# Windowed attention with global tokens, then a squared-ReLU feed-forward layer: matmul width in batch 1, a fourth output buffer, and the order of sums in 256-token chunks

## The chip, the cores and the metric

The kernel runs on one core of a Trainium2 chip. A core has five engines that run side by side[...]: TensorE (PE in the profile, with its weight loads listed apart as PEld), VectorE (DVE), ScalarE (ACT), GpSimd (POOL) and SyncE (SP), which here only issues DMAs. Sixteen DMA engines move data between HBM and the on-chip memory (SBUF). TensorE writes its results to PSUM[...]. The metric is the device time of one execution in microseconds (us); lower is better.

## The reference

Queries, keys and values have 8 batches, 8 heads, 576 tokens and 64 elements per head. A token attends to tokens within 32 positions; 8 global tokens attend to all and are attended by all.

```python
scores = scale * np.matmul(q, k.transpose(0, 1, 3, 2))
mask = np.abs(pos[:, None] - pos[None, :]) <= window        # window = 32
mask = mask | is_global[:, None] | is_global[None, :]
scores = np.where(mask, scores, -1000000000.0)
attn = np.exp(scores - np.max(scores, axis=-1, keepdims=True))
attn_out = np.matmul(attn / (np.sum(attn, axis=-1, keepdims=True) + 1e-09), v)
x = attn_out.transpose(0, 2, 1, 3).reshape(B * S, H * D)    # 4608 x 512
h = x @ w_in                                                # 512 x 2048
r = np.maximum(h, 0.0)
out = (r * r) @ w_out                                       # 2048 x 512
```

## The kernel before

**Attention.** The work is cut into 32 items: item i is a pair of heads of one batch, four items to a batch (`NHP`). Each item has two halves of 288 queries. For an item's half, `sc_mm` (matmuls at L765) makes scores of keys by queries, a head on each 64 rows of the array; `sc_exp` (L774) takes the exponential on ACT, `sc_mask` (L784) multiplies by the 0/1 mask on DVE; `pv_mm` (L806) makes the products with the values and with ones, a head on each 64 columns of the array; `pv_rec`, `pv_sum` and `pv_mul` (L816 to L847) divide and write the result, transposed, into `xT`. `scatter` (L868, POOL) puts in the columns of the global tokens. In batches 0 and 1 keys and queries are loaded as rows and turned round on TensorE by `transpose` (L487; a small product at L493, recorded as L293, picks the global rows); in half 0 of batch 1 the mask is added on TensorE, as a product of `far` with the identity. From batch 2 on, keys and queries go through a scratch in HBM (`kscr`, `qscr`) and come back through transposing DMAs (L201, L202) issued on SP; values come by DMAs on POOL (L207).

**Feed-forward.** The tokens are cut into ten chunks, eight of 512 tokens and two of 256, chunk 4 and the last, chunk 9. `mm1` and, for chunk 0, `mm1_half` multiply by `w_in`; ACT takes the ReLU (`rl`, L538), DVE squares it (`gt`, L540). For chunk 0, `mm2` multiplies by `w_out` directly: four results of 128 tokens, each in four parts; the last part copies the result from PSUM to the tile `ot` (L589) and stores it (L591). All later chunks use `mm2_fast`, which needs seven half-size products in place of eight, in the order 3, 4, 5, 2, 1, 6, 7. Products 5, 2, 1, 6 and 7 read sums or differences of blocks of `gt`, made by `g_sum` on DVE (L625, in tile `mix`) at places that `SUMS` and `SUMS_HALF` set: each entry names the step after which a sum is issued. In `SUMS_HALF` steps 8 to 14 are the seven products. Products are put together by `combine` (L657 into `pt`, L660 into `ot` with a store); product 6 adds onto the bank of product 3 and product 7, in chunk 4, onto that of product 4, so each waits until a combination has read that bank.

**Order.** Every engine takes its instructions in the order in which the program writes them. The attention items set the frame; between their steps `fill(n)` takes feed-forward steps from one list, so that TensorE has work while ACT and DVE do exponentials and masks. A step is only taken when its tokens' batches are done. At the end `take` empties the list. In PSUM, `at` has two buffers of two banks and, from L989 on, `mm` has four of one bank. `ot` has three buffers in SBUF, used in turn.

**How a matmul is issued.** `halves` (L291) issues each product as two matmuls of 64 columns of weights, one for each half of the output's partitions. `transpose` does the same. All such matmuls are recorded under L293 and L487.

## Time and profile before

| | |
|---|---|
| median of 9 runs | 333.19 us (329.68 to 338.06) |
| the profiled execution | 330.38 us |
| its span, first to last instruction | 328.7 us |
| granted TensorE clock, mean | 0.994 |
| PE busy | 309.7 us, 94% of the span |
| DVE, ACT, POOL busy | 244.7, 202.3, 127.1 us |
| DMA moved | 39.35 MB, 120 GB/s |

A line of the profile's groups or timeline names the engine, the line of the kernel, the operation, the tile written and the tiles read, the shape as partitions x elements, and how many. In the timeline the first two numbers are the start and the length in us; a bracket holds the engine's idle time before it and what ended that wait: another engine's instruction, a DMA, or "issue" where nothing in the profile released it. Matmuls overlap, so the busy time of a group is less than its count times its mean. "128*64" is a matmul with 128 rows and 64 columns of weights. In a table of stages a line gives the stretch and its length, then busy time and number of instructions for PE, PEld, DVE, ACT and POOL, the granted clock, the busy share of DMA (where queues overlap it can be over 1) and GB/s.

### The profile page before, as it was taken

The page shows a single profiled execution, that of the slowest core. Times are in us where ns is not written, and L with a number is a line of the kernel's source. Part 1 is how long each engine was busy: PE and PEld are TensorE (multiplying, and loading weights), DVE is VectorE, ACT ScalarE, POOL GpSimd, SP SyncE. Part 2 cuts the span into 40 slices and gives each one's busy share as a digit, 9 for nine tenths or more (in the row PEclk, how much of TensorE's full clock was granted, in tenths as well). Part 3 has the DMA queues.
Part 4 walks back from the last instruction along what each step waited for, and adds up shares of the span by engine and source line. Part 5 has one row for each costly group of instructions (what it writes and reads, how often), then busy time and mean ns, then how long its engine had stood idle before and what let it go on. Part 6 is the DMA issues. An engine that isn't in the chain of part 4 may idle for free.

```text
span 328.7 us, 12010 instructions
## 1 busy us (share of the span) xinstructions
PE 309.7 (94%) x5015; PEld 238.0 (72%) x5015; DVE 244.7 (74%) x601; ACT 202.3 (62%) x380; POOL 127.1 (39%) x222
## 2 busy tenths in 40 slices
PE   7887898998999999999999899999999999999995
PEld 4667786554578758875899756985698569868994
DVE  6783768557898778677867769876987698768465
ACT  3683776544865686668557288658765876363150
POOL 8468767348800960189100970039502000100000
PEclk9997999999999999999999999999999999999999
DMA  8999999999992999499924699469996401200211
GB/s 192 176 182 202 199 190 154 155 117 176 155 118 61 175 157 130 71 177 147 142 79 103 57 181 139 40 130 172 139 98 116 125 0 35 94 5 2 89 45 64
DMA packets 149921, 39.35 MB, mean 120 GB/s; under 512 B 133124, under 2 KB 149300, under 8 KB 149868
## 3 DMA queue, kind: packets, MB, share of 16 engines
q0 software_dynamic: 95408, 16.78, 66.9%
q1 hardware_dynamic: 54042, 21.23, 35.9%
q8 instruction: 39, 0.64, 0.8%
q10 hardware_dynamic: 418, 0.59, 0.7%
q14 instruction: 14, 0.11, 0.1%
HBM read 37.86 MB, written 17.29 MB: 168 GB/s over the span
## 4 chain that ended last, share of the span: by engine, by line
PE 38%; DMA 22%; issue 22%; DVE 7%; POOL 5%; ACT 3%; SPq 1%; POOLq 0%; DVEq 0%
PE mm L293 34%; DMA early<-in_v_dram 9%; DMA w_in<-in_moe_w_in_dram 4%; DMA qscr<-in_q_dram 3%; PE at L806 2%; ACT er L774 2%; PE at L765 2%; POOL xT L868 2%; DMA qt<-qscr 2%; DVE mix L625 2%; DMA gscr_q<-gstq 2%; DMA stf<-in_v_dram 2%; DVE early L619 1%; DVE gt L540 1%; DMA out_dram<-ot 1%
## 5 line engine op out<-in xcount | busy, mean ns | idle before, releaser
L293 PE MATMUL mm<-xT,w_in 128*64 128x512 f16 (+1 forms) x1280 | 123.0, 347 | 2.1 <-DVE ot L589 1.3
L293 PEld LDWEIGHTS <-w_in 128*64 128x64 f16 x1408 | 82.0, 111 | 46.3 <-issue 5.8
L538 ACT ACTIVATE rl<-mm 128x512 f16<-128x512 f32 x128 | 75.0, 598 | 37.5 <-PE mm L293 35.5
L293 PEld LDWEIGHTS <-mix 128*64 128x64 f16 x1280 | 68.5, 110 | 3.5 <-DVE mix L625 1.7
L540 DVE TENSOR_TENSOR gt<-rl 128x512 f16<-128x512 f16 x128 | 52.8, 421 | 22.4 <-ACT rl L538 21.1
L868 POOL COPY xT<-gx 128x4 f16 x64 | 17.7, 277 | 133.4 <-DVE xT L847 130.0
L774 ACT ACTIVATE er<-at 128x880 f16<-128x880 f32 x54 | 46.1, 903 | 15.0 <-PE at L765 13.4
L625 DVE TENSOR_TENSOR mix<-gt 128x1024 f16<-128x1024 f16 (+1 forms) x82 | 53.1, 671 | 0.2
L293 PE MATMUL mm<-early,mix 128*64 128x256 f16 x768 | 45.8, 273 | 1.2 <-DVE mix L625 1.2
L784 DVE TENSOR_TENSOR et<-er,mask 128x880 f16<-128x880 f16 x54 | 33.2, 617 | 17.8 <-ACT er L774 17.3
L816 ACT ACTIVATE rec<-at 128x288 f32<-128x288 f32 x64 | 25.8, 403 | 27.2 <-PE at L806 22.1
L293 PEld LDWEIGHTS <-gt 128*64 128x64 f16 x640 | 34.4, 110 | 8.5 <-DVE gt L540 2.2
L847 DVE TENSOR_TENSOR xT<-at,rec 128x288 f16<-128x288 f32 x60 | 27.1, 451 | 9.1 <-ACT rec L817 8.5
L293 PE MATMUL mm<-early,gt 128*64 128x256 f16 x512 | 32.2, 274 | 1.0 <-DVE gt L540 1.0
L293 PE MATMUL mm<-w_out,mix 128*64 128x256 f16 x512 | 30.9, 273 | 0.0
L806 PE MATMUL at<-et,onesb 128*64 128x192 f16 (+5 forms) x400 | 29.9, 225 | 0.0
L817 ACT ACTIVATE rec<-rec 128x288 f32<-128x288 f32 x64 | 28.4, 443 | 2.0
L660 DVE TENSOR_TENSOR ot<-mm,pt 128x512 f32<-128x512 f32 (+1 forms) x36 | 22.7, 631 | 8.1 <-ACT pt L685 6.7
L178 POOL DMA_DIRECT2D kscr<-in_k_dram x30 | 26.3, 1052 | 3.3 <-DMA w_out<-in_moe_w_out_dram 3.0
L185 POOL DMA_DIRECT2D qscr<-in_q_dram x24 | 23.9, 1398 | 0.6 <-issue 0.6
L806 PEld LDWEIGHTS <-onesb 128*64 128x64 f16 x400 | 22.0, 110 | 1.0
L685 ACT COPY pt<-mm 128x512 f32<-128x512 f32 (+1 forms) x18 | 9.7, 540 | 20.6 <-PE mm L293 20.6
(119 smaller groups left out, 326.9 us busy)
## 6 DMA issues: line engine op xcount, KB each, us to landing
out_dram<-ot SPq DMA_DIRECT2D x32, 256.0 KB
qscr<-in_q_dram POOLq DMA_DIRECT2D x24, 144.0 KB, 8.8
kscr<-in_k_dram POOLq DMA_DIRECT2D x24, 120.0 KB, 6.6
w_in<-in_moe_w_in_dram POOLq DMA_DIRECT2D x4, 512.0 KB, 9.5
w_out<-in_moe_w_out_dram POOLq DMA_DIRECT2D x4, 512.0 KB, 13.9
stf<-in_v_dram POOLq DMA_DIRECT2D x12, 120.0 KB, 12.2
s16b<-in_v_dram POOLq DMA_DIRECT2D x12, 120.0 KB, 9.8
early<-in_v_dram SPq DMA_DIRECT2D x20, 60.0 KB
```

Of the source, the lines that this page charges most:

```text
L178: nc.gpsimd.dma_start(out=kscr[b][r0 : r0 + KN[t]].rearrange("s (h d) -> s h d", d=D), in_=k[b, :, KT * t : KT * t + KN[t]].rearrange("h s ...
L293: nc.tensor.matmul(to[r], weights[:, r], moving, **flags)
L538: nc.scalar.activation(out=rl, in_=ph, func=AF.Relu)
L540: nc.vector.tensor_tensor(out=gt[:, :, 0:T], in0=rl, in1=rl, op=ALU.mult)
L625: nc.vector.tensor_tensor(out=gsums[p][:, lo:hi, 0:TH], in0=g[0], in1=g[1], op=op)
L774: nc.scalar.activation(out=er[:, :, 0:W], in_=scs.pop((i, half))[:, :, 0:W], func=AF.Exp, bias=0.0, scale=scale)
L784: nc.vector.tensor_tensor(out=et[:, :, 0:W], in0=er[:, :, 0:W], in1=mask[:, MB[half] : MB[half] + W].unsqueeze(1).to_broadcast((P, 2, W)), ...
L806: nc.tensor.matmul(acc[D * e : D * e + D, x, o : o + w], onesb if x else vt[:, t, e], et[:, e, so : so + w], start=(n == 0), stop=(n == le ...
L816: nc.scalar.activation(out=rec, in_=av[:, 1, :, 0:GTOK], func=AF.Ln)
L817: nc.scalar.activation(out=rec, in_=rec, func=AF.Exp, scale=-1.0)
L847: nc.vector.tensor_tensor(out=(xT if x0 else xA)[:, hp, x0 : x0 + HS].rearrange("p (k x) -> p k x", k=2), in0=av[:, 0, :, 0:GTOK], in1=rec ...
L868: nc.gpsimd.tensor_copy(out=xb[:, :, ds(gv[g], 1)], in_=gxs[b][:, pairs, g : g + 1])
```

## The change

Three edits. A flag `wide` is set from the point where `mm` gets four banks (late in batch 0) to the last fill of batch 1. While it is set, `halves` and `transpose` issue one matmul of 128 columns in place of two of 64. The tile `ot` gets a fourth buffer. In `SUMS_HALF` the sums for products 1, 6 and 7 are issued earlier: 1 after product 4 (with that for 2), 6 and 7 after product 5, where they were issued after products 5, 2 and 1. A step can now issue two sums.

```diff
+    wide = [False]
+
+    def column_tiles():
+        return (slice(0, P),) if wide[0] else (slice(0, D), slice(D, P))
+
     def halves(to, weights, moving, **flags):
-        for r in (slice(0, P // 2), slice(P // 2, P)):
+        for r in column_tiles():
             nc.tensor.matmul(to[r], weights[:, r], moving, **flags)
...
         for j in range(TJ):
-            for r in (slice(0, D), slice(D, P)):
+            for r in column_tiles():
                 nc.tensor.transpose(
...
-    SUMS_HALF = {5: (5, 0, 4), 8: (5, 4, 8), 9: (2, 0, 8), 10: (1, 0, 8), 11: (6, 0, 8), 12: (7, 0, 8)}
+    SUMS_HALF = {5: (5, 0, 4), 8: (5, 4, 8), 9: (2, 0, 8), 9.5: (1, 0, 8), 10: (6, 0, 8), 10.5: (7, 0, 8)}
 
     def sums_at(c, x):
         plan = SUMS_HALF if CHUNKS[c][1] < TC else SUMS
-        return (plan[x],) if x in plan else ()
+        return [plan[y] for y in (x, x + 0.5) if y in plan]
...
-            ot = sbt("ot", [P, dm], FP32, bufs=3)
+            ot = sbt("ot", [P, dm], FP32, bufs=4)
...
-        t = sbt("ot", [P, dm], FP32, bufs=3).rearrange("p (s m) -> p s m", s=2)[:, 0:n]
+        t = sbt("ot", [P, dm], FP32, bufs=4).rearrange("p (s m) -> p s m", s=2)[:, 0:n]
...
     open_psum(2, 4)
+    wide[0] = True
     for u in range(0, 8, 2):
         mm1_half(u, 0, range(NDM - 1))
...
     fill(3)
+    wide[0] = False
 
     for i in range(2 * NHP, B * NHP):
```

## The prediction

> **What bounds the kernel now.** First the page's busy table, then the table of busy time by stage, which tells where TensorE (PE) has any slack.

> ```profile
> span 328.7 us, 12010 instructions
> ...
> PE 309.7 (94%) x5015; PEld 238.0 (72%) x5015; DVE 244.7 (74%) x601; ACT 202.3 (62%) x380; POOL 127.1 (39%) x222
> ```

> ```profile
> 24.60:36.00 11.40, 8.18 (x128) 7.58 (x129) 4.33 (x11) 6.23 (x15) 9.05 (x26) 0.85 1.30 202
> 36.00:70.70 34.70, 31.71 (x622) 23.56 (x618) 24.33 (x74) 21.22 (x42) 19.50 (x28) 1.00 1.62 163
> 70.70:90.00 19.30, 17.99 (x212) 10.09 (x214) 14.65 (x28) 12.37 (x23) 16.86 (x23) 1.00 1.45 159
> ```

> ```profile
> 90.00:150.00 60.00, 59.36 (x936) 46.13 (x930) 48.79 (x113) 41.34 (x76) 24.62 (x40) 1.00 1.39 131
> 150.00:220.00 70.00, 68.19 (x1120) 54.61 (x1118) 54.42 (x124) 45.34 (x83) 24.26 (x36) 1.00 1.11 111
> 220.00:280.00 60.00, 59.54 (x920) 43.77 (x916) 48.93 (x109) 42.86 (x79) 15.51 (x26) 1.00 0.87 96
> ```

> The second number is PE's busy time. From 90 us on PE is idle for hundredths of a stage, so whatever PE gains after about 71 us should arrive at the end of the span. Before that it has waits, and DMA is full (share 1.62 of one). The kernel divides into a DMA-fed start, up to the first scores of batch 2 at 70.70, and a PE-bound rest. Next I looked in PE's timeline for every place where it stops.

> ```profile
> 44.02 0.38 PE L293 MATMUL mm<-xT,w_in 128*64 128x256 f16 x3 [0.51 <-issue]
> ...
> 50.49 0.33 PE L293 MATMUL mm<-ohp,natq 96*64 96x8 f16 x11 [0.80 <-issue]
> ...
> 57.51 0.20 PE L293 MATMUL mm<-ohp,natk 96*64 96x8 f16 x3 [0.62 <-issue]
> ...
> 70.70 0.56 PE L765 MATMUL at<-qt,kt 64*128 64x160 f16 x12 [0.35 <-DMA qt<-qscr]
> ```

> Three stops in batch 1 wait for no semaphore. Between the first and the second, and between the second and the third, lie exactly 256 PE instructions (loads and matmuls counted in the trace). The page's queue for instructions moved 0.64 MB in 39 packets, 16.4 KB each, which is 256 instructions if one takes 64 bytes. I read them as PE running out of fetched instructions while DMA is full. The last line is the wall: batch 2's first scores wait for a transposing DMA.

> ```profile
> 75.64 1.88 DVE L589 COPY ot<-mm 128x512 f32<-128x512 f32 x3
> ...
> 80.59 0.69 DVE L589 COPY ot<-mm 128x512 f32<-128x512 f32 x1 [2.15 <-DMA out_dram<-ot]
> 81.20 1.42 DVE L540 TENSOR_TENSOR gt<-rl 128x512 f16<-128x512 f16 x4
> 81.33 1.05 PE L293 MATMUL mm<-xT,w_in 128*64 128x512 f16 x8 [1.31 <-DVE ot L589]
> ```

> VectorE (DVE) copies three of chunk 0's four results, then sits until the first store lands and frees an "ot" buffer. PE needs the bank of the fourth.

> ```profile
> 186.05 0.68 DVE L625 TENSOR_TENSOR mix<-gt 128x1024 f16<-128x1024 f16 x1
> ...
> 186.79 2.00 PE L293 MATMUL mm<-early,mix 128*64 128x256 f16 x32 [0.98 <-DVE mix L625]
> ```

> ```profile
> 323.31 0.68 DVE L625 TENSOR_TENSOR mix<-gt 128x1024 f16<-128x1024 f16 x1
> ...
> 324.04 1.06 PE L293 MATMUL mm<-early,mix 128*64 128x256 f16 x16 [0.17 <-DVE mix L625]
> ```

> Both times PE waits for a sum (L625) of a 256-token chunk: chunk 4, and chunk 9, the last.

> **Fourth buffer.** The fourth copy no longer waits. DVE's copies take 0.605 us each from 75.64, so it ends near 78.1 instead of 81.28. PE's 32 halves before the stop are 16 pairs; the last pair starts at 79.64 and streams 0.215, so the next could start at 79.85 instead of 81.33: 1.48 us less. The copy now stands ahead of two reductions and two products of batch 2, which end 0.6 us later, near 79.05. Their reader is the "at" bank of the next scores, which PE reaches at 80.84: covered, by 1.8 us. On SP's queue the fourth store moves up by about 3 us, and batch 3's scratch stores behind it move up too. DVE stays the tight engine up to 94.87, where PE waits 0.41 for it, but its masks there wait for ACT, and ACT for PE's scores at 82.32; all of it moves along.

> **Sums of chunk 4.** Now sum 1 is issued with sum 2, and sums 6 and 7 straight after product 5, ahead of batch 4's first masks. DVE ends sum 1 at 183.01 and idles to 183.90; sums 6 and 7, at 0.605 each, fill 183.0 to 184.2. What queues behind: the combination at 183.90 moves to about 184.15. It releases the bank that product 6 needs at 185.63, so it has a microsecond of cover. The two masks wait for ACT until 184.72 anyhow. Product 1 starts at 184.76 and has 8 pairs of 0.109, so product 6 can start at 185.63 instead of 186.79: 1.16 us. Product 7, 0.87 later, needs a combination that will end near 186.47, against 186.50: no margin, at most 0.1 us.

> **Sums of chunk 9.** DVE would do all five in a row from 319.19 to 321.95. The combination at 321.70 moves to 321.95, ends near 322.4, and product 6 needs its bank at 322.83. Product 7 can start when product 6 has streamed, 321.96 + 16 x 0.109 = 323.71, instead of 324.04: 0.33 us. Its last product, combination and store follow at their old lengths. Four results leave here within 3.5 us; with three buffers the fourth could not start before the first store landed, so the fourth buffer is part of this sum.

> **Full width in batch 1.** No 128-wide, 128-row matmul is in the trace, so its cost is bounded. Affected behind the 1.2 us wait at 35.17 (what stands before it is covered by that wait) are 96 matmuls of 256 columns, 44 of 512, 48 transposes of 96, 48 of 8, and 8 of 440: 244 in place of 488 halves.

> ```profile
> 42.13 0.42 PE L487 MATMUL mm<-identity,natq 96*64 96x96 f16 x12
> 42.39 0.33 PE L293 MATMUL mm<-ohp,natq 96*64 96x8 f16 x12
> 42.58 0.93 PE L293 MATMUL mm<-xT,w_in 128*64 128x256 f16 x13
> ```

> Six pairs of transposes start within 0.26 us, 43 ns a pair, and 96 columns at full clock are 40: halves already run two at a time at streaming rate. So a full-width matmul saves no streaming; its cost lies between zero and an unhidden weight load. The nearest row is L765's 64x128 load of all columns: the second pair of loads starts 11 ns behind the first, under matmuls on the same rows that are still running, and its matmuls follow at 83 ns for 192 columns, which is streaming. Full-width loads hide there. [...]

> Divided value products now lie between undivided ones. [...] The trace shows its price: between 64-row scores and halves the next start is about 98 ns later than streaming one way and 92 the other, and once, from a 1x128 matmul to halves, 88. Batch 1 gets 14 more such changes, 12 of them behind 35.17: 12 x 0.095 = 1.14 us added (from 0, if full to half needs none).

> Against that stand 488 fewer of 1240 PE instructions from 36.0 to 70.7. The three stops beyond streaming cost 0.67, 0.94 and 0.76, sum 2.37 us. 4.8 blocks of 256 become 2.9; at the same share of stops that saves about 0.95 (bounds 0 and 2.37). Net: PE reaches batch 2 about 0.2 us later (1.14 later to 2.4 earlier). It has 0.3 us of wait for the DMA there, and an earlier arrival only waits longer: the key and value transfers that end in that DMA are throttled by DMA itself and wait for no matmul of batch 1. So this part changes the time by 0, at worst by +0.8 unless loads are exposed.

> **Sum.** 1.48 + 1.16 + 0.33 = 2.97 us less. The profiled execution took 330.38 (span 328.7 and 1.7 around it): 327.4. The median of the runs is 2.81 above it; the same microseconds give 330.2. A measurement of this kernel can tell about 1% from no change, 3.3 us, so this lies at that border.

> **Rivals.**
> 1. *Loads are exposed* (slower). [...] From 12.7 ns a matmul on, the change is slower than before. [...] Against: L765's loads. Chance 0.10.
> 2. *A new wait takes the place of one removed.* After 79.85 PE meets DVE, which has weight sums (2.35 us) and squares up to 94.87; if squares are late there, the first 1.48 is lost: 331.7. Against: DVE idles before and is gated by PE's scores. Or a fetch stop falls elsewhere, +0.7. Chance 0.20.
> 3. *The wall moves.* If the DMA that ends at 70.56 comes earlier, because PE fetches fewer blocks, PE keeps 1 to 1.2 us of its stops: 329.1. Against: the chain of waits to it is stores and loads alone. Chance 0.15.
> 4. *The forecast*, 330.2, its own range 328.5 to 332. Chance 0.55.

> Faster by over 1% (below 329.9): 0.17 of the forecast's cases, most of rival 3's, together with runs that scatter low, 0.38. Slower by over 1%: most of rival 1 and a rest, 0.10. Within: 0.52. The range leaves out the exposed-load end and a little below: 327.5 to 334.5.

> **What would show it.** Of the profile after: no wait of L589 for a store, and PE without a stop between 79 and 82; no stop over 0.2 us ahead of products 6 and 7 in either 256-token chunk; full-width matmuls 109 ns (256 columns) and 43 ns (96) apart; fewer issue stops in batch 1; and still a wait for "qt" at about 70.6 ahead of batch 2. Wide spacing there, or scores of batch 2 starting well past 71, would make the prediction wrong; scores at 69 would make it too cautious.

## The result and the profile after

The changed kernel takes 328.22 us, median of 10 runs (326.27 to 330.78), against 332.49 for the kernel before, median of 31 runs (329.68 to 338.06). The ratio is 0.9886, with an interval of 0.9851 to 0.9922: 1.1% faster. Ratios here compare fast runs alone, without those more than 1.5% above the fastest of their kernel, so that they can differ a little from the quotient of the medians. The profiled execution took 327.74 us.

The page's busy table of the changed kernel:

```profile
span 325.9 us, 11457 instructions
...
PE 310.4 (95%) x4739; PEld 235.0 (72%) x4739; DVE 244.8 (75%) x601; ACT 202.2 (62%) x380; POOL 127.8 (39%) x222
```

PE has 276 matmuls and 276 loads fewer and is busy for 0.7 us more (full-width matmuls of 256 columns start 108.6 ns apart here, as pairs of halves did: 109); what went is idle time. By stage, with the columns of the table of before:

```profile
36.00:70.70 34.70, 32.79 (x388) 21.43 (x387) 25.57 (x77) 22.99 (x46) 20.90 (x30) 1.00 1.64 164
70.70:90.00 19.30, 19.15 (x224) 10.73 (x226) 16.09 (x31) 13.71 (x25) 17.03 (x22) 1.00 1.53 171
...
150.00:220.00 70.00, 69.17 (x1154) 56.72 (x1152) 56.06 (x126) 44.84 (x84) 25.26 (x39) 1.00 1.08 112
```

PE idles for 0.15 us in 70.7 to 90, where it had 1.31, and for 0.83 us in 150 to 220, where it had 1.81. In 36 to 70.7 it idles for 1.91 us instead of 2.99. That stage still ends at the same place, although batch 1 began 1.9 us later here (its first transposes at 39.28 against 37.37). PE's timeline shows all three:

```profile
70.85 0.56 PE L770 MATMUL at<-qt,kt 64*128 64x160 f16 x12 [0.48 <-DMA qt<-qscr]
...
76.53 4.51 PE L298 MATMUL mm<-xT,w_in 128*64 128x512 f16 x40
80.97 0.55 PE L770 MATMUL at<-qt,kt 64*128 64x160 f16 x12
...
183.53 2.83 PE L298 MATMUL mm<-early,mix 128*64 128x256 f16 x48
...
319.52 2.79 PE L298 MATMUL mm<-early,mix 128*64 128x256 f16 x48
```

Batch 2's first scores still wait for the transposing DMA, at 70.85 instead of 70.70. The 40 halves from 76.53 run without the stop that stood at 81.33, and in chunks 4 and 9 products 1, 6 and 7 (48 halves) follow one another without a bracket. DVE's timeline has the other side of it:

```profile
75.79 1.88 DVE L594 COPY ot<-mm 128x512 f32<-128x512 f32 x3
...
78.52 0.68 DVE L594 COPY ot<-mm 128x512 f32<-128x512 f32 x1
...
180.14 2.83 DVE L630 TENSOR_TENSOR mix<-gt 128x512 f16<-128x512 f16 x5
...
316.75 2.83 DVE L630 TENSOR_TENSOR mix<-gt 128x512 f16<-128x512 f16 x5
```

The fourth copy waits for no store, and the sums of the two short chunks are made in one go (x5 is the second half of the sum for product 5 and those for 2, 1, 6 and 7). Last, PE's groups with the shapes kept apart, between 37 and 90 us:

```profile
L298 PE MATMUL mm<-w_out,gt 128*128 128x512 f16 x44 | 10.7, 380 | 0.0
L298 PE MATMUL mm<-xT,w_in 128*128 128x256 f16 x64 | 8.0, 273 | 0.0
...
L492 PE MATMUL mm<-identity,natk 96*128 96x96 f16 x24 | 1.7, 207 | 0.3 <-DVE natk L455 0.3
```

A full-width matmul has the mean duration of a half (380, 274 and 206 ns before), and but for 0.3 us ahead of the first keys none of these waits. In the trace their starts are 108.6 ns apart for 256 columns, 42 to 43 for a transpose of 96 and 24 to 25 for the product of 8, where pairs of halves took 109, 43 and 31.

### The profile page after: what moved, and what is told of

The parts are those of the page before. It is cut to its first block, busy times and chain, and to the rows that moved or that the text cites. A ratio compares the mean times of both kernels' runs of the same rounds, so it can differ in the third digit from the quotient of the medians.

```text
span 325.9 us, 11457 instructions
## 1 busy us (share of the span) xinstructions
PE 310.4 (95%) x4739; PEld 235.0 (72%) x4739; DVE 244.8 (75%) x601; ACT 202.2 (62%) x380; POOL 127.8 (39%) x222
## 4 chain that ended last, share of the span: by engine, by line
issue 36%; PE 30%; POOL 12%; DMA 5%; DVE 4%; ACT 2%; POOLq 1%; SPq 0%; ACTq 0%
PE mm L298 25%; POOL kscr L178 3%; DMA qscr<-in_q_dram 3%; POOL xT L873 3%; DMA qt<-qscr 2%; PE at L811 2%; POOL s16b L207 2%; POOL qscr L185 2%; PE at L770 1%; DVE gt L545 1%; ACT er L779 1%; DVE mix L630 1%; PE mm L492 1%; DVE early L624 1%; POOL stf L207 1%
## 5 line engine op out<-in xcount | busy, mean ns | idle before, releaser
L298 PE MATMUL mm<-xT,w_in 128*64 128x512 f16 (+2 forms) x1216 | 122.5, 351 | 0.2 <-POOL xT L873 0.2
L298 PEld LDWEIGHTS <-w_in 128*64 128x64 f16 (+1 forms) x1280 | 80.0, 109 | 45.6 <-issue 3.4
L298 PEld LDWEIGHTS <-gt 128*64 128x64 f16 (+1 forms) x596 | 33.1, 109 | 9.8 <-DVE gt L545 2.2
```

The lines of the kernel that those rows point to most:

```text
L298: nc.tensor.matmul(to[r], weights[:, r], moving, **flags)
```

## The experiments

Two figures of the traces serve all of them. The *stretch of batch 1* runs from its first transposes of keys to the first scores of batch 2. The *rest* runs from those scores to the end of the span: 257.97 us before, 255.06 after. Most gaps between medians are near the width of the intervals, so the traces carry the mechanism and the times its size.

**One part at a time.** e1 has the flag alone, e2 everything but the flag, e3 the fourth buffer alone, e4 the sums alone.

```diff
 # e1: before, and
+    wide[0] = True          # and False after batch 1's last fill
 # e2: after, but without
-    wide[0] = True
 # e3: before, and, at both places
-            ot = sbt("ot", [P, dm], FP32, bufs=3)
+            ot = sbt("ot", [P, dm], FP32, bufs=4)
 # e4: before, and the new SUMS_HALF with sums_at
```

> Only the undivided matmuls of batch 1; three buffers and the old order of sums. Theory A (fetch stops vary from execution to execution; full width only shortens batch 1, and the DMA in front of batch 2 takes what is saved unless an execution reaches it late): the profile keeps the wait of the fourth copy (1.3 us of PE near 81) and of chunk 4 (1.0 us), scores of batch 2 start within 0.4 us of 70.7, and no stop without a releaser stands between 37 and 70; the median falls by 0 to 1.5 us, to a ratio of 0.995 to 1.000. Rival B (full width is worth nothing, the wall always hides it): ratio 0.999 to 1.002. Rival C (the 12 added mode changes cost more than the stops): ratio 1.002 to 1.006.

> The changed kernel without the undivided matmuls. By the sum of the prediction the two other parts are worth 2.97 us: ratio 0.991. Theory A: the rest of the measured 1.14% belongs to full width, so this one stands at 0.990 to 0.993. Rival B: it is as fast as the changed kernel, 0.9885. In the profile PE should again show stops without a releaser at places that are 256 instructions apart, in batch 0 or batch 1.

> Only the fourth buffer. The wait of 1.3 to 1.5 us of PE near 81 goes and those of the sums stay: 1.48 us less, ratio 0.9955. A rival (the squares on DVE become late instead) gives 1.000, with a new wait of PE for L540 between 82 and 95.

> Only the earlier sums, three buffers. Chunk 4 gives 1.16 us. At the end product 7 is 0.33 us earlier, but the fourth result of the last chunk needs the buffer whose store was issued about 2.4 us before: I expect a wait of DVE of 0.3 to 1 us for a store there, so that the end gains nothing or loses up to 0.5. Sum 0.7 to 1.2 us less, ratio 0.9965 to 0.998. If stores land in time, 1.5 us and 0.9955.

| | median, us | ratio to before, interval | at equal clock, us |
|---|---|---|---|
| e1, full width alone | 331.74 | 0.9989 (0.9961 to 1.0016) | -1.1 (-2.3 to +0.2) |
| e2, all but full width | 329.77 | 0.9932 (0.9898 to 0.9966) | -2.6 (-3.5 to -0.6) |
| e3, fourth buffer alone | 331.29 | 0.9972 (0.9946 to 0.9999) | -1.4 (-2.0 to -0.7) |
| e4, sums alone | 332.34 | 0.9980 (0.9950 to 1.0009) | -1.2 (-2.2 to +0.9) |
| the change | 328.22 | 0.9886 (0.9851 to 0.9922) | -3.8 (-4.5 to -2.9) |

The last column compares medians of those runs alone whose mean granted clock was between 0.990 and 0.996 (51 of the kernel before, 7 to 12 of the others; the change with a second set of runs of it, e9), because over all runs the time falls by about 2 us for each 0.01 of clock; its intervals are from resampling those runs. Its parts add up: 1.4 + 1.2 is e2's 2.6, and with e1's 1.1 that is 3.7 of 3.8. So full width is worth about 1.1 us here, where I had forecast nothing. Its own interval, and that of the change against e2 (-1.3 us, -3.0 to 0.0), just reach zero; that two comparisons give the same size, and that the traces below show the mechanism, is what makes me take it as real. That the parts add up so closely is in part luck, as each interval is a microsecond or more wide.

In e1's profiled execution the forecast of nothing holds. Its PE timeline:

```profile
51.68 0.26 PE L811 MATMUL at<-et,early 128*64 128x160 f16 x2 [1.43 <-DVE xT L852]
...
71.33 0.56 PE L770 MATMUL at<-qt,kt 64*128 64x160 f16 x12 [1.45 <-DMA qt<-qscr]
...
81.15 1.05 PE L298 MATMUL mm<-xT,w_in 128*64 128x512 f16 x8 [0.37 <-DVE ot L594]
```

PE came 1.5 us early and waited that long. It had waited 1.43 us already at 51.68, for a result that DVE made late; DVE had itself waited 1.93 us for a DMA of values (L463). e9 and e10, full width too, lose 0.90 and 0.98 us there, and so does e2 (0.89 us), with halves. The stop at the fourth copy, which I expected to stay at 1.3 us, was 0.37 us here. In e3's profile the forecast doesn't hold:

```profile
53.83 0.33 PE L298 MATMUL mm<-ohp,natq 96*64 96x8 f16 x11 [0.86 <-issue]
...
72.80 0.56 PE L770 MATMUL at<-qt,kt 64*128 64x160 f16 x12
...
78.48 4.51 PE L298 MATMUL mm<-xT,w_in 128*64 128x512 f16 x40
```

Here batch 1 began 2.9 us later than in the kernel before (40.30 against 37.37), the halves have their stops without a releaser, and the line of 72.80 has no bracket: the DMA was there already, and PE came last. The line of 78.48 shows the buffer's part at work. Which of the two comes last, PE or the DMA, changes from execution to execution. Where it was PE, the stretch of batch 1 can be read without that DMA. One table row each for e3 and e4 (halves) and e8 (full width, below), from first transposes to first scores:

```profile
40.30:72.80 32.50, 30.62 (x600) 22.99 (x601) 22.66 (x70) 19.89 (x39) 18.56 (x24) 1.00 1.65 168
```

```profile
39.42:71.63 32.21, 31.07 (x601) 22.85 (x602) 22.58 (x70) 19.41 (x39) 17.24 (x24) 1.00 1.66 159
```

```profile
39.02:70.05 31.03, 30.83 (x373) 19.98 (x374) 22.93 (x70) 19.53 (x39) 18.84 (x24) 1.00 1.65 164
```

32.50 and 32.21 us against 31.03, all at full clock (31.02 and 31.03 in e5 and e6, the two other full-width ones in which PE came last). Full width shortens batch 1 by 1.2 to 1.5 us here. All four profiles of halves (before, e2, e3, e4) have two or three stops without a releaser in this stretch, 0.7 to 1.9 us together, and all eight with full width (after, e1, e5 to e10) have none.

The trace tells what becomes of the rest. Add up the times from each start to the next for the transposes, the products of 8 columns and those of `xT` with `w_in`: 12.65 to 13.35 us in the four profiles of halves, 10.6 in each of the eight with full width. So full width saves 2.05 to 2.75 us there. Nearly all of it is gaps between starts, of which the idle time shows a part; the 6 ns saved at each product of 8 columns are small beside them. Everything else in the stretch takes 0.9 us more (20.43 in e8 against 19.54 and 19.56 in e3 and e4), and the 12 more changes of tiling, 1.1 us at the price found below, are the cause that fits; that is an estimate, from the number of changes. The gain of 1.2 to 1.5 us is the difference. It reaches the end when batch 1 starts late or the DMA comes early, and is lost in a wait for a DMA otherwise. In the first profile of the changed kernel batch 1 started 1.9 us late, so that full width paid for the late start; the kernel before would have lost it in the wait.

e4 missed what I had expected of it twice. The stop at the fourth copy, still there with three buffers, was longer this time, as PE's timeline and the stage behind it show:

```profile
83.07 1.05 PE L298 MATMUL mm<-xT,w_in 128*64 128x512 f16 x8 [2.11 <-DVE ot L594]
84.05 0.92 PE L770 MATMUL at<-qt,kt 64*128 64x160 f16 x12
```

```profile
84.00:88.00 4.00, 4.00 (x32) 2.02 (x32) 3.01 (x6) 2.79 (x4) 4.00 (x6) 0.57 1.54 166
```

2.11 us instead of 1.31, and then a granted clock of 0.57 for four microseconds: the 12 scores took 0.92 us instead of 0.56. With three buffers the stop was thus 0.37 (e1), 1.31 (before) or 2.11 us (e4), so that its removal is worth less or more from one execution to the next. And at the end, where I expected a store to be waited for with three buffers, DVE's timeline has none:

```profile
321.17 2.83 DVE L630 TENSOR_TENSOR mix<-gt 128x512 f16<-128x512 f16 x5
...
326.36 0.84 DVE L665 TENSOR_TENSOR ot<-mm,pt 128x256 f32<-128x256 f32 x2
```

The fourth buffer isn't needed for the sums of chunk 9.

e3's time fits the 1.48 us expected (its ratio of 0.9972 has both 0.9955 and nearly 1 in its interval), but its profile shows the rival at work. The next scores come 10.12 us after the first ones, against 11.62 before: 1.50 us gained. Then PE waits for squares:

```profile
96.23 2.05 PE L298 MATMUL mm<-early,gt 128*64 128x256 f16 x34 [0.97 <-DVE gt L545]
...
159.93 0.30 PE L298 MATMUL mm<-early,gt 128*64 128x256 f16 x2 [0.63 <-DVE gt L545]
```

At the first place the kernel before waited 0.24 us, at the second not at all (e1, with three buffers, waits 0.63 us at the second, so that the buffer can't be the whole cause). e3's rest is 257.89 us, as before: in this execution nearly all of the gain was given back. What makes the squares late is the last question below. e2 missed in part as well: at 0.9932 it is just above the 0.990 to 0.993 expected, and of its three stops in batch 1 only one lies on the 256 instructions expected (below).

**More instructions for the same products.** If the stops without a releaser come from the number of PE instructions, then more instructions for the same products must bring more of them. e11 is the kernel before with batch 1 in four tiles of 32 columns, 1104 PE instructions more.

```diff
     def column_tiles():
-        return (slice(0, P),) if wide[0] else (slice(0, D), slice(D, P))
+        return tuple(slice(32 * n, 32 * n + 32) for n in range(4)) if wide[0] else (slice(0, D), slice(D, P))
```

> The kernel before with batch 1's products split four ways (32 columns) where the change has them whole: the same number of mode changes as full width, the same streaming, but 1104 PE instructions more instead of 552 fewer. If PE's stops go by the number of instructions (one block of 256 at a time), batch 1 from 36 to 71 us has 8.7 blocks instead of 4.8; at the stops seen before, 0.6 of the blocks and 0.79 us each, that is 1.8 us more, and 1.1 us of mode changes, less 0.3 of slack: batch 2 starts 2.5 us later, up to 5 if every block stops; ratio 1.008 to 1.016, and the stops lie 256 instructions apart. If the number of instructions doesn't matter, only the mode changes show: 1.002 to 1.004.

Measured: 348.13 us, ratio 1.0489 (1.0424 to 1.0554), about 16 us, three times the most that I expected. PE's timeline names it:

```profile
42.75 0.20 PE L492 MATMUL mm<-identity,natq 96*32 96x96 f16 x1 [2.87 <-issue]
...
49.22 0.40 PE L298 MATMUL mm<-xT,w_in 128*32 128x256 f16 x7 [1.17 <-issue]
...
56.51 0.62 PE L298 MATMUL mm<-xT,w_in 128*32 128x256 f16 x7 [5.30 <-issue]
...
67.26 1.05 PE L298 MATMUL mm<-xT,w_in 128*32 128x256 f16 x16 [2.59 <-issue]
```

They are the PE instructions number 1473, 1729, 1985 and 2497, counted from the start: the first three are the numbers at which the kernel before stopped, though other work stands there now, and the fourth is 512 further. Between them lies 256 or twice that. The four sum to 11.9 us. The stage around the longest:

```profile
52.00:60.00 8.00, 3.49 (x57) 2.33 (x60) 2.31 (x7) 2.15 (x4) 5.61 (x7) 0.58 1.98 156
```

The clock there is 0.58 while DMA's share is 1.98. The stretch of batch 1 is 48.9 us at a mean clock of 0.86, and the rest after it is 258.0, as before: all of the loss lies in batch 1. 11.9 us are stops; the other 4 to 5 us I put down to the lower clock and, for about 1 us, to the 12 more changes of tiling (an estimate: 12 x 0.095). So the place of these stops is set by the count of instructions. The trace also has the transfers of PE's instruction queue, 16,384 bytes each, one for each 256 PE instructions (39 before, 43 in e11, 25 in e5). In none of the thirteen profiles does PE start a block sooner than 1.26 us after its transfer ended, and each of the stops without a releaser at these numbers ends 1.26 to 1.56 us after it: the stop of 5.30 us ends at 56.51, and the transfer ran from 54.08 to 55.04. So I read these stops as PE waiting for its instructions. At most blocks nothing shows: of the 38 of the kernel before that have a transfer of their own in the trace, 34 start 2.4 to 14.9 us after it; the three of these stops and the block of 449 start 1.29 to 1.48 us after it. What I hadn't foreseen is the length: 0.51 to 0.80 us of idle time before, 1.17 to 5.30 when the blocks are used up faster. The trace has the reason in the time from block to block. From the block that begins with instruction 1217 to the next three it is 5.87, 6.47 and 7.02 us before and 5.79, 6.47 and 7.29 in e11: in this stage the transfers set the pace, and PE waits longer when it has less to do with a block. At full width a block there lasts 9 to 12 us, and no transfer is late. Not all stops without a releaser are explained by it: the shorter two of e2 (0.20 and 0.48 us) and of e3 (0.19 and 0.52 us, at instructions 1375 and 1385) and the two of e4 (0.32 and 0.36 us, at 1343 and 1348), and one each of e2 and e7 in batch 0, have no such number. Those of batch 1 stand beside a transfer of PE's queue (from 44.75 to 45.70 in e3, with stops that end at 45.24 and 46.03), but why PE stops there isn't shown.

**The price of a change of tiling.** e5 is the changed kernel with full width left on to the end. That adds 48 changes between full-width matmuls and the divided scores and value products (142 in the trace against 94).

```diff
     fill(3)
-    wide[0] = False
```

> The changed kernel with the flag left on to the end. From batch 2 on the value products (64 columns) then lie between full-width products: two more mode changes in each of 24 items, at 0.095 us each 4.6 us, nearly all on PE's path as PE is the bound there, less where PE waits for DVE anyway. Full-width products themselves stream as before and their loads are hidden. So 3.5 to 4.6 us above the changed kernel: ratio to the kernel before 1.000 to 1.004. If mode changes between full and half width were free, 0.989; if loads at full width show in dense stretches, above 1.01.

Measured: 331.16 us, ratio to before 0.9986 (0.9960 to 1.0013), some 2.5 us slower than the changed kernel at equal clock, less than expected. The rest is 258.42 us in the profiled execution, 3.4 more than after. In the trace each change of tiling costs 92 to 99 ns beyond streaming, whichever two of the three tilings (64 rows by 128 columns, 128 by 64, 128 by 128) it lies between: 48 x 0.095 = 4.6 us. The difference is in PE's waits from 71.5 to 322 us, the changed kernel first (each line: what waits, for what, us in total, times, longest), then e5:

```profile
PE mm L298 <- DVE gt L545: 1.0, 3, 0.4
PE at L770 <- DVE xT L852: 0.9, 2, 0.5
PE at L811 <- DVE et L789: 0.4, 2, 0.2
PE mm L298 <- POOL xT L873: 0.2, 1, 0.2
```

```profile
PE at L770 <- DVE xT L852: 0.7, 2, 0.3
PE mm L298 <- DVE gt L545: 0.4, 1, 0.4
```

2.5 us of waits became 1.1: 1.4 of the 4.6 us fall into waits that PE had anyway, and 3.2 remain, near the 3.4. So some added work was hidden here even with PE busy for 99% of its time (69.17 of 70 us from 150 to 220 in the changed kernel).

**Can it go further?** e6 sets full width from the first instruction, with 252 PE instructions fewer. e7 is the changed kernel with eight idle matmuls in batch 0's last wait, meant to keep the clock up. e8 has both. e9 is the changed kernel itself, beside them on the same chip.

```diff
 # e6, e8
-    wide = [False]
+    wide = [True]
 # e7, e8: after sc_mm(3, 1)
+    warm(pst("mm", [P, 512]), 8)
```

> The changed kernel with the flag set from the first instruction, so batch 0's transposes, mask products and idle matmuls are undivided too: 252 PE instructions fewer, about one block of 256. If stops for instructions (and the half clock that follows a long one) are what full width saves, batch 0 loses part of its stops (seen near 16 and 22 us in several executions), executions reach batch 2 later than the DMA less often, and the median falls by a further 0.3 to 1.5 us; the lowest time stays within 0.7 us of the changed kernel's, since the DMA in front of batch 2 bounds it. If full width works by something else (streaming, loads), batch 0 would be faster or slower in every execution, the lowest time too; if added mode changes cost more than stops, it is slower by up to 1 us.

> The changed kernel with eight idle matmuls of 512 columns put where PE waits near 26 us, ahead of chunk 0's first products. If the half clock near 28 to 34 us makes executions late, the granted clock there rises from 0.5 to near 1 and executions reach the products of batch 1 up to 2 us earlier; the median falls by 0 to 1 us, no more, as the DMA ahead of batch 2 bounds what can be had. If that clock doesn't matter, the time stays within 0.3 us.

> Both of the two before: undivided from the first instruction, and the eight idle matmuls. If both reduce late arrivals at batch 2, it is the fastest of the four, 0.5 to 2 us below the changed kernel in the median, with a narrower spread, and not below its lowest time by more than 0.7 us.

> The changed kernel once more, beside the next three on one chip: ratio 0.985 to 0.992.

Measured: e6 330.13 (0.9902, 0.9865 to 0.9939), e7 329.66 (0.9898, 0.9844 to 0.9952), e8 329.70 (0.9914, 0.9890 to 0.9938), e9 329.07 (0.9899, 0.9850 to 0.9948). None differs from the changed kernel, so that the further gain expected of e6 to e8 isn't there. In e7's profile the clock is full from 24 to 36 us (1.00), as expected, but in e5's, without the idle matmuls, it is 0.9 or more there too (its page), and the time did not follow. e8, the one with most runs, is the nearest to e2's 0.9932, which is one more reason to take the 1.1 us for full width as a rough size. In these profiles batch 1's first transposes start anywhere from 38.7 to 42.3 us, as batch 0's own stops fall, and more than these edits moved.

**What is given back in the rest.** The rest is 255.06 us in the first profile of the changed kernel, but 256.29 in e9's, the same program. ACT's timeline of e9 and then PE's:

```profile
78.78 0.60 ACT L543 ACTIVATE rl<-mm 128x512 f16<-128x512 f32 x1 [0.27 <-issue]
80.02 0.60 ACT L543 ACTIVATE rl<-mm 128x512 f16<-128x512 f32 x1 [0.64 <-PE mm L298]
81.48 1.09 ACT L543 ACTIVATE rl<-mm 128x512 f16<-128x512 f32 x2 [0.87 <-PE mm L298]
```

```profile
94.42 2.05 PE L298 MATMUL mm<-early,gt 128*64 128x256 f16 x34 [0.85 <-DVE gt L545]
```

The ReLUs should start every 0.86 us, as PE delivers; two come 0.4 and 1.0 us late, and PE later waits 0.85 us for their squares, where it waited 0.25 in the first profile. A second such place is near 148 and 158 us. At both, POOL is issuing the indirect DMAs that gather the global rows (L435, items 9 and 17). e10 moves these to items 11 and 19.

```diff
-        if i in (2 * NHP + 1, 4 * NHP + 1):
+        if i in (2 * NHP + 3, 4 * NHP + 3):
```

> The changed kernel with the two later gathers of global rows (POOL, three indirect DMAs each) issued at items 11 and 19 instead of 9 and 17. In most executions profiled so far ACT starts two ReLUs 0.4 to 1.0 us late just while these gathers run (near 80 and 148 us), and PE then waits 0.6 to 0.75 us longer for squares near 94 and 0.5 us near 158. If the gathers cause it, both waits go back to the 0.5 us (94) and below 0.4 (158) of the first profile, ACT is late elsewhere where DVE or nothing waits for it, and the time falls by 0.5 to 1.2 us against the changed kernel, to a ratio of 0.986 to 0.9885 to the kernel before. If they only coincide, ACT is late at the same ReLUs and the time stays at 0.989 to 0.991.

Measured: 329.27 us, ratio 0.9898 (0.9836 to 0.9961), as the changed kernel. In its profiled execution ACT is on time there:

```profile
81.50 0.60 ACT L543 ACTIVATE rl<-mm 128x512 f16<-128x512 f32 x1 [0.27 <-PE mm L298]
82.37 0.60 ACT L543 ACTIVATE rl<-mm 128x512 f16<-128x512 f32 x1 [0.27 <-PE mm L298]
```

and the rest is 255.03. But the first profile of the changed kernel, with the gathers at their old place, had no late start either, and the median didn't move. So the gathers stay a suspicion. In e2, e6, e7, e8 and e9, which keep them at their place, the rest is 255.9 to 256.6: 0.9 to 1.6 us of the gain can be lost this way, and in e3, where ReLUs near 82 and 150 us are late too, 1.4. What makes ACT late isn't settled.

## Why the prediction was right, and where it was off

The time, 328.2 us, lies in the range of 327.5 to 334.5, on the fast side of the forecast of 330.2. The sign was right. At -1.1% it fell just past the border between "within 1%" and "faster", which had 0.52 and 0.38.

1. *Fourth buffer, 1.48 us.* Right for the stop. Measured from batch 2's first scores, the next scores (80.97 against 82.32) start 1.50 us sooner, and e3 gives 1.4 at equal clock. What the sum left out is that one execution showed neither the size of the stop (0.37 us in e1, 2.11 with a clock of 0.57 behind it in e4) nor what comes after: in e3's profile PE waits for squares and the gain is gone by the end.
2. *Sums of chunk 4, 1.16 us.* Right. Product 6 starts 0.87 us behind product 1 (8 pairs of 0.109 in the unbroken 48), where it was 2.03 behind (184.76 and 186.79).
3. *Sums of chunk 9, 0.33 us.* Right in size: the 48 halves from 319.52 have no gap, where 2.08 us lay between the starts of products 1 and 7 (321.96 and 324.04) and 16 pairs stream in 1.74. The three terms together: the rest shrank by 2.91 us between the first profiles, against 2.97 forecast. The condition of this one, that this needs the fourth buffer, fell in e4.
4. *Full width, "by 0".* This is the mis-sized term: about 1.1 us faster at equal clock, 1.2 to 1.5 in the stretch of batch 1. Two things failed in it. I forecast that PE would reach batch 2 "about 0.2 us later", having scaled the stops with the number of blocks (2.37 to 1.42); in fact all of them went, and with four tiles (e11) they became longer as well as more, since the transfers (5.79 to 7.29 us from block to block), and not a share of the blocks, set the pace. And I took the wait for the DMA at 70.7, seen in one execution, for a fixed wall; in e3, e4, e5, e6 and e8 PE came after it, and there each microsecond of batch 1 counts. That the two first profiles reach batch 2 within 0.15 us of each other, as forecast, is luck: the later start of batch 1 hid what full width had gained.
5. *The price of a change of tiling, 0.095 us.* Right: 92 to 99 ns from and to full width, a kind of change that the trace of before had hardly shown.
6. *Loads hidden or exposed.* The row of L765 was right. Transposes of 96 columns at full width, each with its own load, start 42 to 43 ns apart, as pairs of halves did; at the 0.42 ns a column of the pairs of 512 (215 ns) that is 40 ns of streaming. Matmuls of 256 columns start 108.6 ns apart, against 109 for pairs. No load shows, and Rival 1 is out. What an exposed load of 128 columns would cost, no trace here shows.
7. *Rival 2, a new wait.* Partly true, unseen in the first profile and present in e3's and e9's: up to 1.6 us, but with late starts on ACT and not shown to come from weight sums on DVE.
8. *Rival 3, the wall moves.* Not as told: the DMA came at about the same time in the first profiles. That PE, not the DMA, is last in e3, e4, e5, e6 and e8 has the same effect.

At equal clock the three terms measured 2.6 us (e2) against 2.97 forecast, and full width adds the rest of the 3.8. The medians of all runs differ by 332.49 - 328.22 = 4.3; what is above 3.8 is less than the intervals can tell. The forecast of 330.2 also stands on the median of the 9 runs before, 333.19, which 31 runs put at 332.49.

## What to carry to other kernels

Before calling a gain hidden behind a wait that one profile shows, look how large the margin is against the scatter of both sides: here a wait of 0.35 us stood ahead of a DMA whose end moved by 3 us between profiles (PE left that wait at 70.70 to 73.87 us in seven of the thirteen), and it hid a gain only in some of them. Count instructions as a resource of their own where DMA queues are full: the same products in fewer, wider matmuls streamed no faster here (108.6 ns for 256 columns, against 109 for a pair), but batch 1 lost its two or three stops without a releaser. With DMA full in batch 1 (share 1.62 in the kernel before), blocks of 256 PE instructions started no less than 4.9 us apart. Where PE is the bound and the array's tiling alternates, keep the tiling that its neighbours have: each change cost about 0.095 us here.
